# Attention output of batch 3 turned by transposing transfers instead of by TensorE

## The chip, the cores and the metric

The kernel runs on one core of one Trainium2 chip. The metric is the device time of one execution in microseconds (us). The kernel before took 360.15 us, the median of three runs from 359.09 to 361.59. A profiled execution of it took 359.25 us; its profile covers a span of 357.5 us, and all times inside the profile count from the start of that span.

The engines are called as the profile calls them: PE is TensorE (PEld its weight loads), ACT is ScalarE, DVE is VectorE, POOL is GpSimd, SP is SyncE. SP does no arithmetic here; it issues transfers, one after the other in the order of the program, and SPq marks its queue in the profile.

## The reference, cut to what matters

Eight batches of eight heads of causal attention with a decay, over 576 tokens with head size 64, followed by a two-layer network with a SiLU between:

```python
# q, k, v: (8, 8, 576, 64)   f: (8, 8, 576)   w_in: (512, 2048)   w_out: (2048, 512)
cum    = np.cumsum(np.log(np.clip(f, 1e-4, 1.0)), axis=-1)
scores = q @ k.T / sqrt(64) + cum[..., :, None] - cum[..., None, :]     # causal: -1e9 above the diagonal
attn   = softmax(scores)                                                # per head
x      = (attn @ v).transpose(0, 2, 1, 3).reshape(4608, 512)            # tokens x (heads * 64)
h      = x @ w_in
out    = (h * sigmoid(h)) @ w_out                                       # (4608, 512), float32
```

The attention works on tokens as rows. The first product of the network (the MLP) needs x turned: the 512 features on the partitions, the tokens along the free dimension. How x is turned for batch 3 is what this case is about.

## The kernel before, in words

**Pairs.** Two heads are taken together as a pair; pair p belongs to batch b = p // 4 and is the (p % 4)-th of that batch, so there are 32 pairs. For a pair, `scores(p, t)` (line 270) makes four score tiles t = 0 to 3 on PE (line 281) into a PSUM pool of two buffers, ACT takes the exponential (line 306) into the tile `uT`, and DVE multiplies the diagonal blocks with a mask (line 320). `attend_rows(p)` (line 337) multiplies the exponentials with v on PE (line 349, tile `avr`) and DVE divides by the row sums (lines 358 and 359) into the token-major tile `xt` of the batch. `xt` has two buffers, for two batches.

**The MLP.** Its tokens are handled in nine groups of 512; a batch has 576 tokens, so groups and batches don't fall together. Group 3 is tokens 1536 to 2047, and batch 3 is tokens 1728 to 2303: group 3 needs the first 320 tokens of batch 3. `m1_chunk(g, fc)` (line 391) makes one of 16 pieces of the hidden layer of group g from the turned `xT` (four matmuls of 512 columns, line 400, then lines 411 and 412 on ACT and DVE); `m2_part(g, tb, part)` (line 419) makes a quarter of the output of 128 tokens (four matmuls, line 425); after the fourth quarter ACT copies the result out of PSUM (line 434) and SP stores it (line 438). Each such piece or quarter is one *unit* of MLP work below.

**Turning x.** For batches 0 to 3, `turn_pair(p)` (line 366) turns a pair's part of `xt` with five PE transposes through PSUM (line 371, tile `tpx`), and ACT copies it into `xT` (line 377). For batches 4 to 7, `turn_batch(b, c)` (line 379) turns 128 tokens of all heads at once with a transposing transfer issued by SP (line 382); a chunk that crosses the border of two groups takes two transfers. Batches with b < `NTURN` go the first way, the others the second.

**Loading and turning q and k.** From batch 3 on, q and k come from memory by transfers issued by POOL (`load_qk`, line 126) into 16 buffers `mp`, and SP turns them with transposing transfers (`turn_qk`, line 135) into `qT` and `kT`. The five token chunks of a batch and two tensors make ten such turns. v comes by transfers from SP (line 118).

**Order of the work.** The program is written out by a planner that runs when the kernel is built; each engine then takes its own instructions in exactly that order. The planner has a clock of its own in rough microseconds (a unit is 0.88, `scores` of a pair 0.7, `attend_rows` 1.2). `pace(p)` says how many units go beside pair p, so that the units whose x is ready last until the next x comes; `work(n)` emits up to n of them, and nothing where none is ready. `m1_ready` is the number of groups whose x counts as ready. A batch turned by PE is ready at once after its last pair; a batch turned by transfers goes through `retire`, which defers the turns and the readiness by the planner's clock:

```python
for c in range(NB):
    defer(2.5 + 1.2 * c, lambda c=c: turn_batch(b, c))
for g in range(b * S // TG, (b + 1) * S // TG):
    c = ((g + 1) * TG - b * S - 1) // P
    defer(6.2 + 1.2 * c, lambda g=g: made(g + 1))
```

`NTURN` is used in a second place, the plan of the q and k turns (line 535). The first two chunks (i == 0) of a batch b are turned four pairs ahead, but 9.0 units of the planner's clock later if the batch two before it has its x turned by transfers:

```python
elif i == 0 and b - 2 >= NTURN:
    add(plan, NPB * b - 4, defer, 9.0, partial(turn_qk, b, c, w))
else:
    add(plan, NPB * b - 4 + min(i, 1), turn_qk, b, c, w)
```

Of the kernel before, what the change touches and what calls it, by code (L numbers as in the profile page):

```python
# [19 lines left out]
def kernel(  # L20
# [52 lines left out]
    opool = ctx.enter_context(tc.tile_pool(name="opool", bufs=4))  # L73
    NEARLY = 2
    RAW = {0: (0, 1), 1: (0, 1), 2: (0,)}
    NTURN = 4
    LAG = 10.0
    MOST = 9.0
    HOLD = 6
# [286 lines left out]
    def turn_pair(p):  # L366
        b, j = divmod(p, NPB)
        tp = big([P, S], BF16, "tpx")
        for c in range(NB):
            n = bs[c]  # L370
            nc.tensor.transpose(  # L371
                tp[:, c * P : c * P + n],
                xtok[b][:n, c, 2 * j : 2 * j + 2, :].rearrange("p h d -> p (h d)"),
                ident_bf[:n, :n],
            )
        for x, at, o, n in x_parts(b * S, (b + 1) * S):
            nc.scalar.copy(out=x[:, j, at : at + n], in_=tp[:, o : o + n])  # L377
# [68 lines left out]
    def spend(t):  # L446
        nonlocal clock, later
        clock += t
        due = [x for x in later if x[0] <= clock]
        later = [x for x in later if x[0] > clock]  # L450
        for _, fn in due:
            fn()
# [15 lines left out]
    def work(n):  # L468
        nonlocal turn_m2
        for _ in range(n):  # L470
            if can_m2() and (turn_m2 or not can_m1()):
                m2_part(*m2_queue.pop(0))
                turn_m2 = False
            elif can_m1():
                m1_chunk(*m1_queue.pop(0))
                turn_m2 = True
            else:
                return
            spend(0.88)
# [40 lines left out]
    def add(to, at, fn, *args):  # L520
        to.setdefault(at, []).append(lambda: fn(*args))

    for b in range(NEARLY, B):
        for i, group in enumerate([(0, 1), (2,), (3, 4)]):
            at = NPB * b - 4 + min(i, 1) if b == NEARLY else NPB * b - 7 + i
            late = 1 if b == NEARLY + 1 and len(RAW[NEARLY]) == 2 else 0
            for c in group:
                for w in range(2):
# [3 lines left out]
                    if b <= NEARLY + 1:  # L532
                        to = min(at + late + (2 if b == NEARLY else 3), NPB * b - 2)
                        add(plan, to, turn_qk, b, c, w)
                    elif i == 0 and b - 2 >= NTURN:
                        add(plan, NPB * b - 4, defer, 9.0, partial(turn_qk, b, c, w))
# [15 lines left out]
    with tc.manual_schedule():  # L552
# [93 lines left out]
        for p in range(NPB, NP):  # L646
# [43 lines left out]
            work(n3)  # L690
            if j > 0 and b < NTURN:
                turn_pair(p - 1)
            if j == NPB - 1:
                attend_rows(p)
                spend(1.2)
                if b < NTURN:
                    work(2)
# [37 lines left out]
```

## Time and profile before

| | |
|---|---|
| runs | 359.09, 360.15, 361.59 us (median 360.15) |
| profiled execution | 359.25 us, span 357.5 us |
| PE busy | 336.3 us (94%) |
| ACT busy | 211.9 us (59%) |
| DVE busy | 191.7 us (54%) |
| POOL busy | 119.6 us (33%) |
| granted PE clock | 1.00 throughout |
| `tpx` transposes on PE (line 371) | 80 (16 pairs of 5), 219 ns in the median |
| copies of turned x on ACT (line 377) | 32, 404 ns in the median |
| transposing transfers of x (line 382) | 22, 1238 ns on SP in the median, 2.4 us to landing |
| transposing transfers of k and q (line 135) | 30 and 25, 4.9 and 3.8 us to landing |

The busy figures are of the profiled execution. A matmul's duration contains its latency; matmuls overlap, so what one costs PE in a stream is read from start to next start. Times "to landing" run from the issue of a transfer to its completion. In lists of work in order of time, the first column is the start, the second the length, both in us, then engine, line, operation, tile written and read, the number of instructions merged, and in brackets idle time before them and what ended it. "issue" is time in which the engine waited for nothing that the profile shows.

### The profile page before, as it was taken

Reading aid. Unit: us, or ns where it says so; the run is one execution under the profiler, and the core shown is the slowest. Engines: PE = TensorE matmul, PEld = TensorE weight load, DVE = VectorE, ACT = ScalarE, POOL = GpSimd, SP = SyncE. Lnnn points to the kernel's source line nnn. Section 1 sums busy time; section 2 is a strip of 40 time slices with the busy share of each in tenths; the row PEclk is TensorE's granted clock in tenths of the full one; section 3 lists DMA queues with packets and bytes.
Section 4 is the critical chain, followed back from the end, with each engine's and each line's share of the span. In section 5 each row is a group of like instructions: output and inputs, shape, how many; then the busy total and the mean of one; then the engine's idle time right before and its main releaser. Section 6 shows DMA issues by size and latency. Waiting matters only on the chain.

```text
span 357.5 us, 7026 instructions
## 1 busy us (share of the span) xinstructions
PE 336.3 (94%) x2656; PEld 168.4 (47%) x2697; DVE 191.7 (54%) x450; ACT 211.9 (59%) x345; POOL 119.6 (33%) x207
## 2 busy tenths in 40 slices
PE   2797989999999999999999999999999999999995
PEld 1455445554555445544454453444444454444442
DVE  4664895538743675348543791567237723744300
ACT  4566674558753986388647764676468615644421
POOL 5563598239554235423564250110301000000000
PEclk9999999999999999999999999999999999999999
DMA  8899999999997998399969994452240014000021
GB/s 220 213 208 315 192 193 222 155 210 170 148 150 117 163 150 78 89 170 142 124 122 152 130 166 123 100 117 75 74 83 31 1 68 118 2 29 29 31 76 71
DMA packets 142514, 44.92 MB, mean 126 GB/s; under 512 B 129616, under 2 KB 136784, under 8 KB 142480
## 3 DMA queue, kind: packets, MB, share of 16 engines
q1 hardware_dynamic: 87664, 33.64, 42.5%
q0 software_dynamic: 54736, 10.69, 38.4%
q8 instruction: 21, 0.34, 0.4%
q10 hardware_dynamic: 80, 0.15, 0.2%
q14 instruction: 13, 0.11, 0.1%
HBM read 36.85 MB, written 9.44 MB: 129 GB/s over the span
## 4 chain that ended last, share of the span: by engine, by line
PE 82%; DVE 6%; ACT 4%; DMA 3%; issue 3%; POOL 1%; SPq 0%; ACTq 0%
PE po L425 33%; PE hp L400 30%; PE avr L349 7%; PE sc L281 7%; DVE gtile L412 2%; ACT uT L306 2%; DMA xT<-xt 2%; PE tpx L371 2%; DVE uT L320 2%; PE tpqk L235 2%; ACT th L411 1%; DMA whole<-in_k_dram 1%; DVE xt L359 1%; PE sc L289 1%; DVE qT L240 1%
## 5 line engine op out<-in xcount | busy, mean ns | idle before, releaser
L400 PE MATMUL hp<-xT,w_in_bf 128*128 128x512 bf16 x556 | 135.8, 380 | 3.2 <-DVE gtile L412 0.8
L425 PE MATMUL po<-w_out_bf,gtile 128*128 128x512 bf16 x555 | 133.7, 379 | 1.4 <-DVE gtile L412 0.4
L412 DVE SCALAR_TENSOR_TENSOR gtile<-th,hp 128x512 bf16<-128x512 bf16 x144 | 96.0, 685 | 52.2 <-ACT th L411 50.3
L306 ACT ACTIVATE uT<-sc 128x1024 bf16<-128x1024 f32 (+1 forms) x128 | 101.3, 850 | 24.9 <-PE sc L281 15.9
L411 ACT ACTIVATE th<-hp 128x512 bf16<-128x512 f32 x144 | 84.8, 613 | 50.0 <-PE hp L400 46.2
L251 POOL TENSOR_TENSOR vaug<-vm,wT 128x512 bf16<-128x512 f32 x64 | 45.4, 729 | 132.7 <-PE avr L349 121.4
L400 PEld LDWEIGHTS <-w_in_bf 128*128 128x128 bf16 x576 | 53.1, 98 | 65.2 <-issue 6.1
L425 PEld LDWEIGHTS <-gtile 128*128 128x128 bf16 x576 | 53.6, 98 | 62.9 <-issue 2.4
L320 DVE TENSOR_TENSOR uT<-uT,mask 128x256 bf16<-128x256 bf16 (+1 forms) x112 | 35.3, 337 | 66.2 <-ACT uT L306 66.0
L434 ACT ACTIVATE osb<-po 128x512 f32<-128x512 f32 x36 | 21.7, 602 | 46.7 <-PE po L425 46.7
L281 PE MATMUL sc<-qT,kT 64*128 64x64 bf16 (+4 forms) x384 | 37.3, 287 | 5.5 <-ACT uT L306 2.2
L349 PEld LDWEIGHTS <-uT 128*128 128x128 bf16 x960 | 33.7, 98 | 6.4 <-issue 0.7
L349 PE MATMUL avr<-vaug,uT 128*128 128x65 bf16 x960 | 36.2, 195 | 0.2 <-POOL vaug L259 0.2
L359 DVE TENSOR_TENSOR xt<-avr,rr 128x384 bf16<-128x384 f32 x64 | 31.4, 491 | 2.3
L281 PEld LDWEIGHTS <-kT 64*128 64x128 bf16 x384 | 15.3, 95 | 30.1 <-issue 21.0
L126 POOL DMA_DIRECT2D mp<-in_k_dram x30 | 25.9, 865 | 1.0 <-DMA mp<-in_k_dram 1.0
L126 POOL DMA_DIRECT2D mp<-in_q_dram x25 | 22.2, 887 | 1.3 <-DMA w_out_bf<-in_moe_w_out_dram 0.5
L358 DVE RECIPROCAL rr<-avr 128x6 f32<-128x6 f32 x64 | 11.7, 183 | 18.6 <-PE avr L349 18.5
L377 ACT COPY xT<-tpx 128x512 bf16<-128x512 bf16 (+7 forms) x32 | 11.2, 404 | 17.0 <-PE tpx L371 16.9
L193 POOL CAST m<-whole 128x512 bf16<-128x512 f32 x20 | 11.9, 607 | 15.0 <-DMA whole<-in_q_dram 12.4
L235 PE MATMUL tpqk<-ident_bf,m 128*128 128x128 bf16 (+1 forms) x90 | 10.9, 241 | 0.3 <-DVE gtile L412 0.3
L235 PEld LDWEIGHTS <-m 128*128 128x128 bf16 (+1 forms) x90 | 7.3, 106 | 6.3 <-issue 1.6
(47 smaller groups left out, 71.8 us busy)
## 6 DMA issues: line engine op xcount, KB each, us to landing
out_dram<-osb SPq DMA_DIRECT2D x36, 256.0 KB, 2.2
vm<-in_v_dram SPq DMA_DIRECT2D x32, 256.0 KB, 4.7
mp<-in_k_dram POOLq DMA_DIRECT2D x24, 128.0 KB, 6.2
whole<-in_q_dram SPq DMA_DIRECT2D x5, 512.0 KB, 9.7
mp<-in_q_dram POOLq DMA_DIRECT2D x20, 128.0 KB, 4.8
w_in_bf<-in_moe_w_in_dram POOLq DMA_DIRECT2D x2, 1024.0 KB, 11.2
w_out_bf<-in_moe_w_out_dram POOLq DMA_DIRECT2D x4, 512.0 KB, 10.7
whole<-in_k_dram SPq DMA_DIRECT2D x3, 512.0 KB, 9.5
```

Of the source, the lines that this page charges most:

```text
L126: nc.gpsimd.dma_start(out=t[: bs[c], :].rearrange("p (h d) -> p h d", h=H), in_=(q, k)[which][b, :, c * P : c * P + bs[c], :].rearrange("h ...
L235: nc.tensor.transpose(tp[:, c * P : c * P + n], m[:n, c, :, :].rearrange("p h d -> p (h d)"), ident_bf[:n, :n],)
L251: nc.gpsimd.tensor_tensor(out=va[:n, c0:c1, :, 0:D], in0=vm[:n, c0:c1, 2 * j : 2 * j + 2, :], in1=wT[:n, c0:c1, 2 * j + b * H : 2 * j + 2 ...
L281: nc.tensor.matmul(sc[:, i, col : col + n], lhsT=kT[r, kb * P : (kb + 1) * P], rhs=qT[r, q0 : q0 + n], start=True, stop=not pe_adds,)
L306: nc.scalar.activation(out=u[:, :, o : o + col], in_=sc[:, :, 0:col], func=ACT.Exp, scale=scale)
L320: nc.vector.tensor_tensor(out=d, in0=d, in1=mk, op=ALU.mult)
L349: nc.tensor.matmul(av[:, qb - lo, i, :], lhsT=u[:, i, o : o + P], rhs=va[:, kb, i, :], start=(kb == 0), stop=(kb == qb),)
L359: nc.vector.tensor_tensor(out=xt[:, lo:hi, 2 * j : 2 * j + 2, :], in0=av[:, :, :, 0:D], in1=r[:, 0:n, :, None].to_broadcast([P, n, 2, D]), ...
L400: nc.tensor.matmul(hp[:, :], lhsT=w_in_bf[:, cc, fc * P : (fc + 1) * P], rhs=xg[g][:, cc, :], start=(cc == 0), stop=(cc == NCC - 1),)
L411: nc.scalar.activation(out=th[:, :], in_=hp[:, :], func=ACT.Tanh, scale=0.5)
L412: nc.vector.scalar_tensor_tensor(out=gte[:, fc, :], in0=th[:, :], scalar=1.0, in1=hp[:, :], op0=ALU.add, op1=ALU.mult,)
L425: nc.tensor.matmul(po[:, :], lhsT=gte[:, fc, tb * P : (tb + 1) * P], rhs=w_out_bf[:, fc, :], start=(fc == 0), stop=(fc == NFC - 1),)
```

## The change

One constant changes:

```diff
     NEARLY = 2
     RAW = {0: (0, 1), 1: (0, 1), 2: (0,)}
-    NTURN = 4
+    NTURN = 3
     LAG = 10.0
     MOST = 9.0
```

It acts in three places. In the main loop, the four `turn_pair` calls of batch 3 (lines 692 and 698) are not made, nor are the two units that `work(2)` placed ahead of the last one; the end of batch 3 calls `retire` instead of `ready`:

```python
if j > 0 and b < NTURN:
    turn_pair(p - 1)
if j == NPB - 1:
    attend_rows(p)
    spend(1.2)
    if b < NTURN:
        work(2)
        turn_pair(p)
        ready(p)
    else:
        retire(p)
```

Batch 3's x is then turned by six transposing transfers on SP (chunk 2, tokens 1984 to 2111, crosses from group 3 to group 4 at token 2048 and takes two), and group 3 counts as ready only after its deferral. In the plan of q and k, the condition of line 535 now holds for batch 5 as well, so its first four turns (q and k of chunks 0 and 1) are emitted 9.0 units of the planner's clock after the start of pair 16 instead of at its start. Through `m1_ready` and `pace`, the number of MLP units beside the pairs after batch 3 changes too; the units themselves and all the arithmetic stay.

## The prediction

> **What bounds the kernel now.** I read the page's busy shares first, then its 40 slices and its chain, then TensorE's (PE's) timeline, and last the queue of the engine that issues the turning transfers (SP).
>
> ```profile
> PE 336.3 (94%) x2656; PEld 168.4 (47%) x2697; DVE 191.7 (54%) x450; ACT 211.9 (59%) x345; POOL 119.6 (33%) x207
> ...
> PE   2797989999999999999999999999999999999995
> ```
>
> PE is full in all but the first and last of the 40 slices; between 60 and 345 us the windows have it busy for 280.5 of 285 us, and the chain that ended last is 82% PE. So a microsecond of PE work removed is a microsecond gained, and one in which PE waits is lost: no later slack takes it up. The question is what PE waits for after the change. The one place where it waits now for an x turned by transfer, at the end of batch 4, is on the chain between 140 and 200 us:
>
> ```profile
> 188.19 0.34 SPq L438
> 188.53 0.06 issue
> 188.59 4.86 DMA xT<-xt
> 193.44 0.05 issue
> 193.49 0.39 PE hp L400
> ```
>
> Columns are start, length and what ran. Just before them ScalarE's output copy ended (187.56 to 188.17); SP then issues that output, and only then the transposing transfer that stood behind it in its list, which lands 4.86 us later; then PE begins the MLP's group 4. SP works strictly in order: its waits for output copies come to 143.8 us in 27 times. PE's timeline there shows that attention alone doesn't fill it; one score tile waits 0.52 us for an exponential:
>
> ```profile
> 191.61 0.21 PE L281 MATMUL sc<-qT,kT 64*128 64x64 bf16 x2 [0.52 <-ACT uT L306]
> 191.74 1.09 PE L349 MATMUL avr<-vaug,uT 128*128 128x65 bf16 x30
> 192.76 0.61 PE L281 MATMUL sc<-qT,kT 64*128 64x512 bf16 x6
> 193.49 1.04 PE L400 MATMUL hp<-xT,w_in_bf 128*128 128x512 bf16 x3
> ```
>
> **Step 1, PE work removed.** The four turns of batch 3, line 371, are five transposes each:
>
> ```profile
> 150.74 0.52 PE L371 MATMUL tpx<-ident_bf,xt 128*128 128x128 bf16 x5
> 151.06 0.63 PE L281 MATMUL sc<-qT,kT 64*128 64x512 bf16 x6
> ```
>
> The durations overlap what follows, so I count from start to next start: 0.32 here, and 0.32, 0.33 and 0.45 for those at 130.16, 138.46 and 147.64: **1.42 us off**. The eight ScalarE copies go as well (404 ns in the median, some 3 us), but ScalarE has slack there (5.1 of 11 us busy from 140 to 151) and PE waits for none of them, so they count nothing.
>
> **Step 2, the MLP's work dries up earlier.** The planner's arithmetic is fixed by the code and can be replayed. Now, group 3 is ready as pair 15 ends, and pairs 16 to 20 get 6, 7, 7, 7, 6 units of MLP work (0.865 us each: four 512-column matmuls at 0.216), pair 21 gets 1 and pair 22 gets 9. After the change, group 3 becomes ready 8.6 planner units after pair 15, so pairs 16, 17, 18 get 4, 1, 0 and pair 19 gets 9. The thin place moves from pair 21 to pairs 16 to 18 and becomes longer. The old one vanishes (later pairs have 19 units or more in stock): 0.52 us before the last score tile and 0.2 before group 4: **0.7 us off**.
>
> In the new one ScalarE is the limit: a pair's exponentials take 3.0 us (four in 3.02 at 189.62), PE's own scores and products of a pair 1.8 (0.54 + 0.35 + 0.91), and only two score tiles exist. Placing them one by one, from the last product of batch 3 (148.09 now, 146.98 after, since three turns of 1.10 are gone): scores 16 to 148.5, four units with the second half of the scores between to 152.3, first scores 17 to 152.85, last unit to 153.7, then every score tile waits for an exponential: scores 18 at 156.2 to 158.5, scores 19 end at 159.95. That is 12.97 us for 10.3 us of work: **2.6 us on** (1.5 if the output copies slip between, 3.2 if the mask steps come late).
>
> **Step 3, SP's queue.** Program order on SP after the output of pair 16: chunks 0 and 1 of batch 3's x; six q/k turns of batch 5 and two v loads; one output; chunk 2 in two pieces, chunks 3 and 4; two v loads; then the other four q/k turns of batch 5, formerly ahead of all this and now deferred. Group 3 ends 320 tokens into batch 3, so it needs the first piece of chunk 2, *behind* the six q/k turns. The same run of six is in the trace:
>
> ```profile
> 158.79 1.23 SPq L135 DMA_TRANSPOSE qT<-mp  x1
> 160.12 1.22 SPq L135 DMA_TRANSPOSE kT<-mp  x1
> 161.42 1.22 SPq L135 DMA_TRANSPOSE qT<-mp  x1
> 162.74 1.22 SPq L135 DMA_TRANSPOSE kT<-mp  x1
> 164.01 0.57 SPq L118 DMA_DIRECT2D vm<-in_v_dram  x1
> ```
>
> One transposing issue every 1.31 us, six with two loads 9.0 us (158.79 to 167.8). The output ahead of it can go at 151.05 (unit done 149.35, ScalarE's two exponentials until 150.3, copy 0.6); chunk 0 at 151.45, chunk 1 at 152.75, q/k turns 154.05 to 163.1, the output 0.35, chunk 2 at 163.5. The x transfers' issues (ns, least, median, most) and landings:
>
> ```profile
> L382 SPq DMA_TRANSPOSE xT<-xt x22: 1171/1238/1671, 183.6 to 300.2; - x22
> ...
> DMA to landing us min/median/max: 2.3/2.4/4.9
> ```
>
> So group 3 can start at 165.9 to 168.4; I take 166.7, nearer the median. PE stands ready at 159.95: 6.7 us. PE has nothing to do meanwhile: all that stands behind the waiting matmul waits with it, and so do ScalarE and VectorE behind PE.
>
> The queue bites again. The last deferred turn (k, chunk 1) comes seven turns (1.31 each) and two loads (0.65) after chunk 2's first piece, at about 174.1. Turns of q and k land 2.3 to 6.3 us after their issue in the stretches I read (medians 3.8 for q and 4.9 for k over the run): 178.6 with 4.5. Pair 20's second score tile needs it. PE gets there 10.2 us after group 3 begins (9 units 7.8, scores and products 2.4): 176.9. Without SP it would have been there at 170.2. The two waits together cost 178.6 - 170.2 = **8.4 us on** (6.4 with the shortest landings, 10.1 with the longest; 2 more if several issues take 1.7 to 2.1 us as around 85 and 123 us). GpSimd's q/k loads of pair 19 also wait for the deferred turns to free their buffers, but batch 6 needs them only at pair 24.
>
> **The sum.** -1.42 - 0.7 + 2.6 + 8.4 = +8.9 us on the profiled execution's 359.25 us (span 357.5 and 1.75 around it): 368.1. That execution lay 0.9 us under the median of the runs shown (360.15), within their spread; I say **368**. All low ends together give +5.8 (365.0), all high ends +13.2 (372.5).
>
> **A rule of the skill that speaks against the change.** The row first: the 512-column score matmul takes 605 ns until 19.8 us and 386 ns from 25.4 us, though the page shows a granted clock of 1.00 throughout; the slow form held through 6 us of work without a gap over 0.2 us (17.74 to 24). The Trainium skill, "TensorE: Matmul & The Clock Gate", section "Part 1: The HAM clock gate", says that TensorE runs at half clock after an idle window of about 3.4 us and regains full speed after a busy one; by it the time would be the second rival's 369.5. No run here shows it: from 100 us to the end of PE's work the longest wait on another engine is 0.52 us.
>
> **Rivals.**
> - *Not slower: chunk 2 in time.* If its first piece lands before 159.95 and the k turn before 170.2, only steps 1 and 2 count: 359.25 - 2.1 + 2.6 = **359.8**; with no exponential waits either, 357.1. It decides where eight turns, two loads and an output fit between 151.45 and about 157.5, half of the 12.05 us that the rows give. For it: SP's rows may be more of waiting than of issuing. Against: the 1.31 spacing in every run of turns, waits or not. Chance 0.1.
> - *A slow clock after the gap.* Waits of 6.7 and 1.7 us are longer than any now. If PE then runs at the rate of the first 20 us (605 against 386 ns, 0.22 us more for a matmul of 0.216) for half or all of 6 us, it reaches pair 20 1.5 to 3 us later, at 178.4 to 179.9; the k turn, due at 178.6, hides most, and a slow start after the second wait adds about as much as the rest: **369.5** (up to 372). Chance 0.25.
> - *Half the queue.* If SP starts its run 3 us sooner or the k turn lands in 2.5 us and the exponentials hide in the wait: -2.1 + 1.5 + 4.5, **363.2**. For it: SP is idle before 151 except for one held output. Against: that output cannot move ahead of its copy. Chance 0.1.
> - The forecast itself, 365 to 371: 0.55.
>
> **Range and chances.** A measurement of this kernel tells about 1% (3.6 us) from no change. The range is 363.5 to 372.5: it holds the forecast, most of the slow-clock case and the edge of the half-queue one. Faster by over 1% (below 355.6) needs more than all removed work with no wait at all: 0.03. Within 1%: 0.12, the first rival and part of the third. Slower: 0.85.
>
> **What would show it.** Line 371 with 60 matmuls instead of 80 and line 382 with 28 transfers instead of 22. The first matmul of line 400 after some 150 us with 5 to 8 us idle before it, released by the x transfer. SP showing chunks 0 and 1 of x, then six turns of line 135, then x again. A second wait of 1 to 3 us on line 281, released by the kT transfer, about 10 us later. After it no gap of size until the end, and the last MLP stretch unchanged. It is wrong if PE waits for neither transfer, if the x turns pass the q/k turns, or if the idle time comes back later.

## The result and the profile after

| | before | after |
|---|---|---|
| median of the runs | 359.70 us (359.09 to 361.59) | 368.73 us (368.01 to 369.45) |
| ratio | 1 | 1.0252, 95% interval 1.0228 to 1.0277 |
| span of the profiled execution | 357.5 us | 366.6 us |
| PE busy | 336.3 us | 337.7 us |
| transposes on PE for x (line 371) | 80 | 60 |
| transposing transfers of x (line 382) | 22 | 28 |

The change costs 9.0 us; 368.0 was forecast. Both medians are of six executions; three of those before are the ones shown ahead of the prediction, with 360.15 as their median. The page of the kernel after, busy shares and slices:

```profile
PE 337.7 (92%) x2637; PEld 168.0 (46%) x2677; DVE 194.2 (53%) x450; ACT 210.3 (57%) x337; POOL 119.7 (33%) x207
...
PE   2798979999999999937999999999999999999995
...
PEclk9999999999999999975999999999999999999999
```

PE does less work than before but is busy for longer (337.7 against 336.3 us), and two things are new: a hole in the two slices from 156 to 174 us, and a granted clock that falls beside it. The waits on PE from 100 us on, total, times and longest:

```profile
PE hp L400 <- DMA xT<-xt: 6.4, 1, 6.4
PE sc L281 <- ACT uT L306: 2.1, 4, 0.9
```

PE's timeline through the hole:

```profile
154.88 0.20 PE L281 MATMUL sc<-qT,kT 64*128 64x64 bf16 x2 [0.52 <-ACT uT L306]
155.02 1.08 PE L349 MATMUL avr<-vaug,uT 128*128 128x65 bf16 x30
156.28 0.61 PE L281 MATMUL sc<-qT,kT 64*128 64x512 bf16 x6 [0.18 <-ACT uT L306]
157.79 0.39 PE L281 MATMUL sc<-qT,kT 64*128 64x320 bf16 x4 [0.89 <-ACT uT L306]
158.70 0.20 PE L281 MATMUL sc<-qT,kT 64*128 64x64 bf16 x2 [0.52 <-ACT uT L306]
158.84 1.27 PE L349 MATMUL avr<-vaug,uT 128*128 128x65 bf16 x30
160.05 1.03 PE L281 MATMUL sc<-qT,kT 64*128 64x512 bf16 x6
167.43 0.58 PE L400 MATMUL hp<-xT,w_in_bf 128*128 128x512 bf16 x1 [6.35 <-DMA xT<-xt]
168.24 4.47 PE L400 MATMUL hp<-xT,w_in_bf 128*128 128x512 bf16 x10 [0.22 <-issue]
```

Pairs 17 and 18 run without MLP work and wait four times for exponentials; then group 3 waits 6.35 us for its x. From the products at 158.84 on, work is slower than its like: thirty products take 1.27 us where they took 1.08, six score matmuls 1.03 instead of 0.61. SP's queue says why x came so late:

```profile
150.78 0.33 SPq L438 DMA_DIRECT2D out_dram<-osb  x1
151.21 2.72 SPq L382 DMA_TRANSPOSE xT<-xt  x2
154.03 1.24 SPq L135 DMA_TRANSPOSE qT<-mp  x1
...
163.71 0.57 SPq L438 DMA_DIRECT2D out_dram<-osb  x1
164.32 5.10 SPq L382 DMA_TRANSPOSE xT<-xt  x4
169.52 1.21 SPq L118 DMA_DIRECT2D vm<-in_v_dram  x2
170.77 2.86 SPq L135 DMA_TRANSPOSE qT<-mp  x1
173.68 1.30 SPq L135 DMA_TRANSPOSE kT<-mp  x1
175.08 1.98 SPq L135 DMA_TRANSPOSE qT<-mp  x1
177.16 1.21 SPq L135 DMA_TRANSPOSE kT<-mp  x1
```

Chunks 0 and 1 of x go out at 151.21, six q and k turns follow, and the piece that group 3 lacks is issued at 164.32. It lands 2.97 us later, as the chain shows:

```profile
164.32 2.97 DMA xT<-xt
167.30 0.14 issue
167.43 0.58 PE hp L400
```

The windows over the same time: length, busy time of PE and (not used here) its weight loads, DVE, ACT, POOL, then the granted clock, the transfers' share and GB/s.

```profile
154.00:159.00 5.00, 2.88 (x54) 2.04 (x54) 3.19 (x8) 4.69 (x7) 2.78 (x5) 1.00 1.91 145
159.00:160.00 1.00, 1.00 (x30) 0.95 (x27) 0.93 (x5) 0.74 (x2) 0.71 (x1) 0.78 1.24 229
160.00:167.40 7.40, 1.08 (x9) 0.28 (x6) 1.92 (x8) 1.94 (x2) 1.61 (x3) 0.50 1.40 184
167.40:173.00 5.60, 5.34 (x15) 1.86 (x18) 1.37 (x2) 1.45 (x3) 3.20 (x4) 0.50 1.14 111
173.00:180.00 7.00, 6.95 (x81) 3.97 (x79) 5.76 (x12) 4.82 (x9) 1.57 (x3) 0.98 1.35 151
```

The clock is halved at about 159.6 (0.78 in the mean from 159 to 160), stays so through the wait and through 5.3 us of matmuls until 173.2, and a 512-column matmul of line 400 takes 627 ns there in the mean against 379 elsewhere. Pair 19 then needs 12.9 us from the first matmul of group 3 to pair 20.

**The account.** Removed: 1.4 us of transposes and 0.7 of the old thin place. Added: 2.1 of waits for exponentials, 6.35 for x, and some 3.4 of slow matmuls (0.2 and 0.4 in the two lines ahead of the wait, 2.8 in pair 19, whose 12.9 us take 10.15 at full clock in experiment 3 below). Together +9.7, against 9.1 between the spans; the 0.6 us between the two are not accounted for. From 180 us on PE waits for no other engine.

### The profile page after: what moved, and what is told of

Read it like the earlier page. It is cut to its first block, busy times and chain, and to the rows that moved or that the text cites. A ratio compares the mean times of both kernels' runs of the same rounds, so it can differ in the third digit from the quotient of the medians.

```text
span 366.6 us, 6994 instructions
## 1 busy us (share of the span) xinstructions
PE 337.7 (92%) x2637; PEld 168.0 (46%) x2677; DVE 194.2 (53%) x450; ACT 210.3 (57%) x337; POOL 119.7 (33%) x207
## 4 chain that ended last, share of the span: by engine, by line
PE 81%; DVE 6%; ACT 4%; issue 3%; SPq 2%; DMA 2%; POOL 0%; ACTq 0%; DVEq 0%
PE po L425 34%; PE hp L400 30%; PE avr L349 7%; PE sc L281 7%; ACT uT L306 2%; DVE gtile L412 2%; SPq L135 2%; DVE uT L320 2%; PE tpqk L235 1%; PE tpx L371 1%; ACT th L411 1%; DMA whole<-in_k_dram 1%; DMA xT<-xt 1%; DVE xt L359 1%; PE sc L289 1%
## 5 line engine op out<-in xcount | busy, mean ns | idle before, releaser
L400 PE MATMUL hp<-xT,w_in_bf 128*128 128x512 bf16 x556 | 140.1, 384 | 9.5 <-DMA xT<-xt 6.4
L425 PE MATMUL po<-w_out_bf,gtile 128*128 128x512 bf16 x556 | 136.2, 379 | 1.3 <-DVE gtile L412 0.4
L400 PEld LDWEIGHTS <-w_in_bf 128*128 128x128 bf16 x576 | 53.9, 99 | 73.1 <-issue 14.6
L320 DVE TENSOR_TENSOR uT<-uT,mask 128x256 bf16<-128x256 bf16 (+1 forms) x112 | 37.5, 358 | 58.2 <-ACT uT L306 57.9
L358 DVE RECIPROCAL rr<-avr 128x6 f32<-128x6 f32 x64 | 11.6, 181 | 13.3 <-PE avr L349 13.3
L377 ACT COPY xT<-tpx 128x512 bf16<-128x512 bf16 (+5 forms) x24 | 8.4, 404 | 10.4 <-PE tpx L371 10.4
```

What stands on the lines that cost most here:

```text
L320: nc.vector.tensor_tensor(out=d, in0=d, in1=mk, op=ALU.mult)
L400: nc.tensor.matmul(hp[:, :], lhsT=w_in_bf[:, cc, fc * P : (fc + 1) * P], rhs=xg[g][:, cc, :], start=(cc == 0), stop=(cc == NCC - 1),)
L425: nc.tensor.matmul(po[:, :], lhsT=gte[:, fc, tb * P : (tb + 1) * P], rhs=w_out_bf[:, fc, :], start=(fc == 0), stop=(fc == NFC - 1),)
```

## The experiments

Two theories stood at the start. **The queue:** SP's list, from the first x chunk at 151.21 to the end of the last deferred turn at 178.4, decides when pair 20 can go on; the wait for x and the slow clock lie inside it. In its favour: the last k turn was issued at 177.16 and landed 2.7 us later, at 179.9, and PE came to pair 20 at 180.34. **The wait for x:** the 6.4 us and the slow clock behind them are the whole cost, and a better order of the same transfers, or a full clock, brings each back. Each ratio below is to executions of the kernel before measured together with the experiment (medians 360.19 to 360.57 us).

### 1. PE kept busy through the holes

```diff
+            if p == 19:
+                warm(26)          # 512-column matmuls into a PSUM tile nobody reads
             work(n1)
...
+            if p in (17, 18):
+                warm(3)
             scores(p, 2)
+            if p in (17, 18):
+                warm(3)
             scores(p, 3)
```

Two more stand ahead of the first scores of pair 18.

> The changed kernel with 40 matmuls whose result nothing reads placed in the places where PE waits: 14 around the scores of pairs 17 and 18, 26 ahead of the first matmul of group 3, so that PE doesn't idle there. By my theory (SP's queue sets when pair 20 can go on: its last k turn lands at 179.9, and PE came to it at 180.3) a granted clock that stays at 1.00 gains 0.5 us at most: 368.0 to 368.9, and a new wait of about 2 us on line 281 for the q or k turn. By the rival (the slow clock costs what it adds to the matmuls of pair 19, 12.9 against 9.9 us, and no transfer stands behind it) the time falls by 3.0 to 365.7, with no wait on line 281.

Measured: 369.43 us, ratio to the kernel before 1.0252 (1.0209 to 1.0296), that of the change itself; no gain at all, where the queue theory allowed up to 0.5 us. The granted clock was 0.998 in the mean. Its PE timeline:

```profile
162.13 5.79 PE L484 MATMUL warm<-w_in_bf 128*128 128x512 bf16 x26
169.63 2.75 PE L400 MATMUL hp<-xT,w_in_bf 128*128 128x512 bf16 x12 [1.71 <-DMA xT<-xt]
...
181.27 0.73 PE L281 MATMUL sc<-qT,kT 64*128 64x512 bf16 x6 [1.43 <-DMA kT<-mp]
```

Twelve matmuls take 2.75 us again, and pair 20 now waits for its k. The full clock is lost to the transfers in the queue. This is what the first theory expects (the new wait 1.4 us, not 2) and not the second. The experiment isn't clean, though: the queue itself ran later than after the change. Group 3 begins at 169.63 instead of 167.43, and the four x pieces hold SP for 6.76 us instead of 5.10; why isn't known.

### 2. The deferred turns in their old place

```diff
-                    elif i == 0 and b - 2 >= NTURN:
+                    elif i == 0 and b - 2 > NTURN:
```

> The changed kernel with the q and k turns of batch 5 in the order of the kernel before: chunks 0 and 1 at the start of pair 16, so ahead of batch 3's x. By the queue theory four turns (5.2 us) more stand before chunk 2 of x: it lands at 172.5 instead of 167.3, the wait of line 400 grows from 6.4 to 11.6 us, pair 20 waits for nothing, the time grows to 373 to 374. If the deferral of these four turns was what hurt (pair 20 waiting for them), it falls to about 367 or below.

Measured: 368.87 us, ratio 1.0240 (1.0188 to 1.0291), the same as the change. Both expectations missed, the wait for x being 6.5 us instead of 11.6. Its SP queue shows what I had overlooked:

```profile
144.49 1.25 SPq L135 DMA_TRANSPOSE qT<-mp  x1
145.84 1.21 SPq L135 DMA_TRANSPOSE kT<-mp  x1
147.14 1.22 SPq L135 DMA_TRANSPOSE qT<-mp  x1
148.45 1.22 SPq L135 DMA_TRANSPOSE kT<-mp  x1
149.72 0.58 SPq L118 DMA_DIRECT2D vm<-in_v_dram  x1
150.60 1.59 SPq L438 DMA_DIRECT2D out_dram<-osb  x1
152.29 2.56 SPq L382 DMA_TRANSPOSE xT<-xt  x2
```

With `work(2)` gone ahead of pair 16, these turns stand in front of the output that SP otherwise waits for until 150.6, and fill an idle stretch. The x chunks follow at 152.29, only 1.1 us later than after the change, and the piece that group 3 needs at 164.92, 0.6 us later. Nothing waits for a k turn here, and still nothing is gained: the slow clock now fills the same time, PE reaching pair 20 at 180.25.

### 3. Both at once

The `warm` lines of experiment 1 together with the edit of experiment 2:

```diff
+                warm(26)
...
-                    elif i == 0 and b - 2 >= NTURN:
+                    elif i == 0 and b - 2 > NTURN:
```

> Both at once of what changed nothing alone: the unread matmuls that keep the granted clock at 1.00, and the four q and k turns of batch 5 in their old place, so that neither a slow clock nor the last k turn stands behind the wait for x. If these two hid each other, the 3.0 us by which pair 19 is slow come back now: 365.5 to 366.5. If the slow clock costs nothing of its own, the time stays at 368.9.

Measured: 367.46 us, ratio 1.0202 (1.0168 to 1.0236). PE needs 10.15 us from group 3 to pair 20 (169.11 to 179.26) and waits for no k; x, however, comes 1.2 us later than in experiment 2 (169.11 against 167.92): the output ahead of it starts 0.4 us later and holds SP for 1.13 us instead of 0.57. So the expected 365.5 to 366.5 was missed, and about half of the 3 us shows in the time. The point estimate lies below those of 1 and 2 but the intervals overlap: that the two covers hid one another is read from the traces (pair 20 reached at 181.27, 180.25 and 179.26), the times alone do not show it.

### 4. The thin place alone

x of batch 3 by PE as before, group 3 called ready as late as after the change.

```diff
+                if b == 3:
+                    turn_pair(p)
+                    defer(8.6, lambda: made(4))
-                if b < NTURN:
+                elif b < NTURN:
```

> The kernel before (x of batch 3 by PE, q and k turns as there) with only the readiness of group 3 delayed by the 8.6 planner units of the change, so pairs 16 to 19 get 4, 1, 0 and 9 units of MLP work. What the thin place costs by itself, with no transfer to wait for: 2.1 us of waits for exponentials come, 0.7 go: 361.1. If the granted clock falls in the thin place as it did at 159.8 after the change, and nothing hides it, about 3 us more: 364.

Measured: 362.97 us against 360.57, ratio 1.0076 (1.0046 to 1.0106), 2.7 us at the ratio. The trace has the 2.1 us of waits for exponentials, at the same four places; the clock falls here too (0.57 in the mean of 164 to 168 us) but recovers soon (the first twelve matmuls of group 3 take 3.15 us against 2.76), and group 4 waits 1.0 us for its x. The profiled execution is the slowest of the ten (366.46 us); it lies 2.7 us behind the kernel before already at the last products of batch 3 (150.77 against 148.09), where the edit hasn't acted yet, so its waits can be read but not its total. The 2.7 us at the ratio lie between the two expectations, 1.4 and 4.3 us above the kernel before. Of the 9 us of the change, the dried-up MLP is therefore at most a bit under a third, since the wait of group 4 and 0.5 us of waits of the last turn of batch 3, which the changed kernel doesn't have, are in it; the rest needs the transfers.

### 5. x ahead of the six turns

```diff
-                        add(plan, NPB * b - 4 + min(i, 1), turn_qk, b, c, w)
+                        add(plan, NPB * b - 4 + (2 if b == 5 else min(i, 1)), turn_qk, b, c, w)
```

> The changed kernel with the six q and k turns of batch 5's chunks 2 to 4 emitted one pair later, behind chunks 0 to 3 of batch 3's x. The same transfers stand on SP, in another order. By the queue theory the wait of line 400 nearly goes (0 to 1 us), but the last k turn still lands at about 180 and pair 20 waits for it instead, 5 to 8 us on line 281: 367 to 369. By the rival (the wait for x is the cost, the order its cause) the 6.4 us come back: 360 to 363.

Measured: 373.47 us, ratio 1.0339 (1.0276 to 1.0401): slower than the change. The waits on PE:

```profile
PE sc L281 <- DMA qT<-mp: 5.6, 1, 5.6
PE sc L281 <- DMA kT<-mp: 2.8, 1, 2.8
PE sc L281 <- ACT uT L306: 2.1, 4, 0.9
PE hp L400 <- DMA xT<-xt: 1.4, 1, 1.4
```

The wait for x shrinks from 6.4 to 1.4 us and 8.4 us appear at pair 20. That is the queue theory's move and rules the other out; the time is 4.5 to 6.5 us above its figure (3 to 5 at the ratio). SP stood for 2.3 us on an output ahead of chunk 2, so the six turns began at 162.88 and the last of the ten ended at 179.9, and the clock fell twice (twelve matmuls in 4.64 and in 4.08 us). This reordering only moved the wait. That PE needs more work beside the queue is argued here, and put to the test in experiments 8 and 9.

### 6. The deferral alone

In the kernel before, with `NTURN` still 4:

```diff
-                    elif i == 0 and b - 2 >= NTURN:
+                    elif i == 0 and b - 2 >= NTURN - 1:
```

> The kernel before (x of batch 3 by PE) with only the second use of the constant changed: the first four q and k turns of batch 5 deferred by 9.0 planner units. They then go out in pair 17, behind the six others, and land some 12 us before pair 20: no difference, 0.997 to 1.003 of the time before. If late turns cost by themselves, 2 us or more with a wait on line 281.

Measured: 359.74 us, ratio 0.9981 (0.9959 to 1.0003): no difference, and no wait on line 281 for a transfer. By itself the second use of the constant is harmless: in this kernel the turns have landed before PE comes to them.

### 7. All ten turns early

```diff
             scores(p, 3)
+            if p == 15:
+                for fn in early5:     # the ten q and k turns of batch 5
+                    fn()
```

> The changed kernel with all ten q and k turns of batch 5 emitted right after the scores of pair 15, so that SP makes them from 142 us on, where it waits now for output copies. By the queue theory both waits for transfers all but go: chunk 2 of x is issued at about 159 and lands at 161.5, PE comes at 161, pair 20 waits for nothing. Left are 2.1 us of exponential waits and a granted clock that falls in the thin place, 1 to 2 us, against 2.1 us of removed work and waits: 360.5 to 362.5. If the x transfers are late for another reason than the six turns ahead of them, the wait for x stays above 4 us and the time above 365.

Measured: 368.51 us, ratio 1.0216 (1.0172 to 1.0259). The wait for x is 6.5 us as before, which I had expected only if something other than the six turns made x late. SP's queue:

```profile
156.23 1.21 SPq L135 DMA_TRANSPOSE kT<-mp  x1
157.53 0.54 SPq L438 DMA_DIRECT2D out_dram<-osb  x1
158.13 0.42 SPq L118 DMA_DIRECT2D vm<-in_v_dram  x1
158.64 0.66 SPq L438 DMA_DIRECT2D out_dram<-osb  x1
159.38 2.53 SPq L382 DMA_TRANSPOSE xT<-xt  x2
161.97 1.24 SPq L118 DMA_DIRECT2D vm<-in_v_dram  x2
163.31 1.28 SPq L438 DMA_DIRECT2D out_dram<-osb  x1
164.63 5.11 SPq L382 DMA_TRANSPOSE xT<-xt  x4
```

It was again the turns ahead of x, now ten of them, from 143.3 to 157.4, with three outputs and three v loads that I hadn't counted: x's piece goes out at 164.63 instead of 159. SP's list has no gap above 0.2 us from 143.3 to 172.4. The measured time lies where I had put the rival cause; it is the list that speaks for the queue here, and experiment 9 that tests it.

### 8. Early turns, and MLP work spread over the gap

Experiment 7 with a lag of 16 in the pace of batch 3 and 3.4 more ahead of its readiness.

> As the kernel with early turns, and the planner told that the x of batch 3 will be later still (a lag of 16 in place of 7 in the pace of batch 3, readiness 3.4 later), so that pairs 12 to 19 get 5, 5, 6, 5, 5, 7, 9, 9 units and none runs without MLP work. Then no exponential is waited for, the clock stays at 1.00, and what is left of the change is the PE work and the old thin place that it removes, 1.4 and 0.7 us: 357.5 to 358.5, 0.6% under the kernel before. If the transfers cost PE in some other way, it stays at 360 or above.

Measured: 372.15 us, ratio 1.0339 (1.0301 to 1.0376), as slow as experiment 5. No exponential is waited for, but the work of pair 17 reaches group 3 at 155.9, before x:

```profile
162.20 1.87 PE L400 MATMUL hp<-xT,w_in_bf 128*128 128x512 bf16 x4 [6.27 <-DMA xT<-xt]
...
197.35 1.86 PE L400 MATMUL hp<-xT,w_in_bf 128*128 128x512 bf16 x4 [3.77 <-issue]
```

The second line is the start of group 4. The trace names no releaser for it, but its x was issued from 189.05 on, behind an output whose copy SP had waited 18.8 us for. Both gaps are followed by slow matmuls, four in 1.87 us. Spreading the work removes the thin place, not the queue ahead of x.

### 9. x at once, ahead of everything

```diff
         for c in range(NB):
-            defer(2.5 + 1.2 * c, lambda c=c: turn_batch(b, c))
+            turn_batch(b, c)
         for g in range(b * S // TG, (b + 1) * S // TG):
             c = ((g + 1) * TG - b * S - 1) // P
-            defer(6.2 + 1.2 * c, lambda g=g: made(g + 1))
+            defer({3: 9.6, 7: 6.2}.get(b, 8.0) + 1.2 * c, lambda g=g: made(g + 1))
```

and the lag of 16 of experiment 8.

> The changed kernel with three edits of the order: the x transfers of a batch are emitted at once after its last pair, ahead of everything later on SP; the pace of batch 3 counts a lag of 16 in place of 7, so pairs 12 to 19 get 5, 5, 6, 5, 5, 7, 9, 9 units; a group counts as ready 8.0 (batch 3: 9.6) units after the last pair plus 1.2 a chunk, in place of 6.2. SP then issues x's six pieces from about 2 us after the last product of batch 3, the piece that group 3 needs lands some 9 us after it, and PE comes to group 3 after 12; the ten q and k turns follow with 20 us to spare. By my theory no transfer and no exponential is waited for, the clock stays at 1.00, and the removed PE work and thin place show at last: 357 to 358.5 (0.992 to 0.996 of the kernel before). If x transfers cost PE in some way beyond the queue and the thin place, the time stays above 360.

Measured: 357.92 us, ratio to the kernel before 0.9921 (0.9898 to 0.9945). As expected. Its whole list of waits on PE from 100 to 345 us, and PE where group 3 begins:

```profile
PE hp L400 <- DVE gtile L412: 0.7, 2, 0.3
```

```profile
154.54 1.07 PE L349 MATMUL avr<-vaug,uT 128*128 128x65 bf16 x30
155.45 1.03 PE L425 MATMUL po<-w_out_bf,gtile 128*128 128x512 bf16 x4
156.31 1.03 PE L400 MATMUL hp<-xT,w_in_bf 128*128 128x512 bf16 x4
```

The six pieces of x go out in one run from 144.16 to 151.92, and the ten turns follow until 171. The clock is 1.00 throughout.

### 10. The control: the same emission in the kernel before

Only the first edit of experiment 9, in the kernel before:

```diff
-            defer(2.5 + 1.2 * c, lambda c=c: turn_batch(b, c))
+            turn_batch(b, c)
```

> Control: the kernel before (x of batch 3 by PE) with the one edit that emits the x transfers of batches 4 to 7 at once after the last pair. Pairs get the same units as before. At most the waits for x there (0.2 and 0.3 us) go: 0.997 to 1.001 of the kernel before. If this reordering by itself brings 1 us or more, a gain of the other kernel of this call is not the change's.

Measured: 359.25 us, ratio 0.9973 (0.9955 to 0.9992). So 0.3% of experiment 9's 0.8% comes with the emission alone, within what was expected; the rest, 0.5%, is the change together with the pacing that it needs (the two intervals just don't meet). In microseconds that is 1.3 between the two medians, near the 1.4 us of transposes removed. No run gave the kernel before the pacing of experiment 9, so how much of the 1.3 us belongs to the pacing is not shown.

## Why the prediction was right

**The work removed** (1.42 us): right. The last products of batch 3 start at 146.89 instead of 148.09, 1.20 earlier where three turns were put at 1.10, and line 371 has 60 matmuls.

**The thin place:** right in place and near in size. PE's order after pair 15 is the one replayed, with 4, 1, 0 and 9 units. Its waits are 2.1 us, 2.6 were forecast; PE ended the scores of pair 19 at 161.1 instead of 159.95, 0.6 us of the difference coming from the clock (0.2 and 0.4 in the account above).

**SP's queue, first part:** right to within a microsecond. Forecast 151.05, 151.45, 154.05 and 163.5 for the output, x, the six turns and the piece of x; the trace has 150.78, 151.21, 154.03 and 164.32. It landed at 167.3 (166.7), and the wait is 6.35 us (6.7).

**SP's queue, second part:** right in its bound, wrong in its form. The last k turn was put at 174.1 with 4.5 us to landing, 178.6; it was issued at 177.16, since two of the turns held SP for 2.86 and 1.98 us where 1.31 was reckoned and the run began 0.8 us late, and landed at 179.9. The wait of 1 to 3 us on line 281 that I named as its sign did not come, because PE itself arrived only at 180.3.

**The slow clock,** the second rival at 0.25: it did come. The row that it was worked out from held (627 against 379 ns for a 512-column matmul), and so did its own remark that the k turn hides most of it: experiment 1 removes it and gains nothing, though there x came 2.2 us later as well. The page's 1.00 ahead of 23.8 us, which the prediction found at odds with its slow matmuls, is no reading: the trace's record of the clock begins only there, and the matmuls become fast at about 24. The rival was wrong on the occasion: the clock fell at 159.6, in the thin place, before the long wait. The Trainium skill's rule ("TensorE: Matmul & The Clock Gate", section "Part 1: The HAM clock gate") that an idle window brings half the clock and busy work of some 3.4 us the full one agrees in its time, but the window before the fall was not an idle one: PE was busy for 1.87 of the 3.41 us up to 159.57, with no wait on another engine above 0.9 us. The full clock came back at 173.22, after the first such stretch that was busy throughout (169.81 to 173.22), 5.8 us from the start of group 3, which had begun within the stretch before.

**The sum:** +8.9 forecast, 9.1 between the profiled spans and 9.0 between the medians. Forecast and rival were 1.5 us apart (368 and 369.5), so the time doesn't decide between them: it is the trace and experiments 1 to 3 that show both causes present, each covering the other. That the sum came out so near is in part luck: its last step, a second wait of 1.7 us, never came, slow matmuls of 3.4 us stood in its place, and PE reached pair 20 1.7 us later than forecast (180.3 against 178.6).

**The rivals that fell:** "not slower" would have needed half the issue time per turn; six turns with two loads took 9.6 us against 9.0 reckoned. "Half the queue" asked for an earlier start of SP's run. Experiment 2 found the idle stretch for it, 144.5 to 150.6, which I hadn't seen as open to the four deferred turns; it did not help x.

## What to carry to other kernels

Work moved from a full engine to an idle transfer queue isn't free when that queue is served in order: read what stands ahead of the new entry, at the issue time per entry (here 1.31 us a turn), and count the outputs and loads as well as the transfers in question. When two delays cover each other, removing one shows nothing; remove both, or look in the trace for what becomes late next. A change that looks bad may need its order changed with it: the same constant costs 2.5% as it stands and gains 0.8% with x issued first and the MLP's work spread over the wait, of which 0.3% comes from the order alone.

## What the runs showed of the hardware

The granted clock fell to 0.50 in a stretch where PE was busy for 2.88 of 5 us in pieces, and it stayed there for 13.65 us, of which 5.3 at the end were dense work. In the kernel before, 2.48 of 3 us busy (189 to 192) left the clock at 1.00.

The clock moved in steps of 3.41 us. The halved stretches in the traces' records last 13.65 us after the change and in experiment 2, 3.41 in experiment 4, 6.83 and 10.24 in experiment 5, 6.83 in experiment 7, 6.83 and 3.41 in experiment 8: all whole multiples of 3.41, and so are the full ones between them (10.24 and 30.72 us). A thin place therefore counts by how these steps cut it. The step that ended with the fall had PE busy for 1.87 us after the change and for 1.81 in experiments 2 and 4. In experiment 7 a border fell into the same thin place and left 2.35 and 2.16 us of work on its two sides; the clock held until 165.6, after a step without any work. So the thirty products at the end of the thin place took 1.27 us after the change, 1.82 in experiment 2, 1.78 in experiment 4 and 1.09 in experiment 7. The clock came back after the first step with 2.98 us or more of work. Busy time alone gives no threshold for the fall: a step with 1.83 us of work in experiment 1, most of it 512-column matmuls, left the clock full.

A transposing transfer of q or k usually holds SP for 1.20 to 1.25 us, but those issued from 170.77 to 177.16 held it for 2.86, 1.30, 1.98 and 1.21 us and landed after 2.7 to 7.7 us. POOL was issuing four q and k loads from 167.55 to 170.75, so these transfers ran beside them; that this is the cause was not tested.
